# A weight conversion by scaling instead of a range check, and a gather of diagonal blocks on ScalarE alone

## The chip, the cores and the metric

The kernel runs on one core of one Trainium2 chip. The metric is the device time of one execution in microseconds (us). Quoted times are medians of several executions. A profile of one execution stands beside them; its span is about 1.8 us shorter than the time of the same execution. A run counts as fast when it is within 1.5% of the fastest of the same kernel, and each comparison is between fast runs. The experiments ran on five chips; the medians of the kernel before on them lie within 0.3 us of each other, so medians are compared across chips too.

Some terms. *Output products* are the matmuls `p_ffn<-w_out,g`, *solve products* the small ones into `p_one` from `diag` or `r`; each product gives two records in the profile. The *stage* is the stretch from the first to the last `g` of the first two chunks, 78 to 158 us in the kernel before. A *slow phase* is a stretch in which TensorE's granted clock is 0.50; in the 17 traces kept here it is 0.50 or 1.00 and nothing else, and a figure between the two is a mean over a longer stretch.

Engines in profile lines: PE is TensorE, PEld its weight loads, DVE VectorE, ACT ScalarE, POOL GpSimd. "L357" is a line of that kernel's program. The changed kernel has fewer lines, so one operation has different numbers in different kernels: kk is L357 before and L349 after, `low` L562 and L553, `g` L565 and L556.

## The reference

A delta-rule attention (batch 4, 8 heads, 768 steps, head size 48) is followed by a feed-forward layer with a PReLU on 3072 tokens.

```
k_n = k / (norm(k) + 1e-6)
for each step t:   y_t = q_t S
                   S   = S + beta_t * k_t (v_t - k_t S)
h   = y W_in                    # 384 -> 2048
out = (max(h,0) + alpha*min(h,0)) W_out
```

The weights arrive as float64. The chip has to make float32 of them from pairs of 32-bit words.

## The kernel before

The attention is worked in chunks of 64 tokens; 24 steps (12 chunks, 2 halves of the batch). Four steps at a time share one *elimination*: the 32x32 diagonal blocks of `kk` are gathered into `same`, turned by a block transpose, and eliminated row by row on VectorE. TensorE runs the feed-forward products (`ffn_in`, `ffn_out`) between the small products of the attention.

```python
# weight conversion, one piece (cut)
nc.scalar.activation(dst.bitcast(U32), lo, ACT.Copy, scale=2.0**-29)   # low word
nc.scalar.square(lo.bitcast(FP32), hi.bitcast(FP32))                    # for the range check
# VectorE, first half
tensor_scalar(out=high, in0=hi, scalar1=3, scalar2=0x3FFFFFF8, shift_left, and)
scalar_tensor_tensor(out=hi, in0=hi, scalar=0xC0000000, in1=high, and, or)
yield
# second half
tensor_tensor(out=dst.bitcast(U32), in0=hi, in1=dst.bitcast(U32), op=add)
scalar_tensor_tensor(out=dst, in0=lo, scalar=LEAST*LEAST, in1=dst, is_ge, mult)
yield

# prep(n): the weight of each key (cut)
nc.scalar.square(ksq, k)                       # ksq has one buffer
nc.vector.tensor_reduce(out=norm, in_=ksq, op=add)
nc.scalar.sqrt(norm, norm)
nc.vector.tensor_scalar_add(norm, norm, 1e-6)
nc.vector.reciprocal(rec, norm)

# keep(n): gather of the diagonal blocks, right after kk
nc.scalar.mul(same[m][:, j], kk[n][:, :, 0:HB], which[:, 0:1])
nc.vector.scalar_tensor_tensor(out=same[m][:, j], in0=kk[n][:, :, HB:C],
    scalar=which[:, 1:2], in1=same[m][:, j], op0=mult, op1=add)
if j == NJ - 1:                                # every fourth step
    nc.vector.transpose(block[m], same[m])

# ffn_in: after each pair of input products
nc.scalar.activation(low, p_h, ACT.Relu, scale=-1.0)
for i in range(2):
    g[:, i] = low[:, i] * al_t + p_h[:, i]     # VectorE

# the opening, in this order (cut)
busy(31)                                       # filler products while VectorE eliminates
eliminate(0)
weave(ready/pair of steps 0,1 with one filler each, 12 half pieces of the conversion)
weave(steps 2,3; conversion; prep, kk, keep of steps 4 to 7; ffn_in(0))
weave(rest of the conversion; ffn_in(1); kk, keep of steps 8, 9)
weave(eliminate(1), ffn_out(0))
place(4); between_1(4); between_2(4); ...      # first products that need elimination 1
# here the fixed order ends; for the rest the build orders instructions itself
```

`weave` interleaves generators at compile time, so each engine has one fixed row of instructions.

## Time and profile before

| | before |
|---|---|
| median of 3 runs | 795.0 us |
| TensorE busy | 95% of the span |
| VectorE, ScalarE busy | 54%, 27% |
| VectorE busy, 120 to 140 us | 19.1 of 20 us |
| TensorE's granted clock after four waits of 2 to 3 us, mean of 4 us | 0.57 to 0.62 (slow phases of 3.41 us) |

The shares of the whole span name TensorE as the bound; the stretches show another bound, VectorE, between 78 and 160 us. The prediction below shows those lines and reads them.

### The profile page before, as it was taken

What the parts mean: (1) busy time and instruction counts of PE and PEld (TensorE: products, weight loads), DVE (VectorE), ACT (ScalarE), POOL (GpSimd) and SP (SyncE); (2) the same over time, 40 slices, a digit from 0 to 9 for tenths busy, and PEclk for the clock granted to TensorE, in tenths of its full rate; (3) what the DMA queues carried; (4) which work ended last, traced back from release to release, by engine and by line L of the source; (5) the groups of instructions that cost most, each with busy time, mean ns of one, the idle gap of its engine ahead of it and who ended that gap; (6) DMA issues with size and microseconds to landing.
All of it is one profiled execution on the core that took longest, in us unless ns stands there. A gap on an engine that the chain in (4) does not pass through costs nothing.

```text
span 792.7 us, 20343 instructions
## 1 busy us (share of the span) xinstructions
PE 755.3 (95%) x8987; PEld 557.1 (70%) x8987; DVE 429.4 (54%) x1007; ACT 215.4 (27%) x443; POOL 23.3 (3%) x80
## 2 busy tenths in 40 slices
PE   5999888698998999999999999999999999999997
PEld 4457666555787678678678678678677687687684
DVE  6997989995599224596234596223595132122030
ACT  3415546412324123124123123123113122021110
POOL 5000000010000000000000000000000000000000
PEclk9999999999999999999999999999999999999999
DMA  7718453211321122122122121111111110100000
GB/s 154 171 41 223 91 138 82 76 26 32 62 45 34 26 41 42 22 41 42 22 41 41 22 42 31 22 32 32 22 32 31 23 38 3 21 12 2 21 0 21
DMA packets 109417, 37.60 MB, mean 47 GB/s; under 512 B 102625, under 2 KB 105713, under 8 KB 109329
## 3 DMA queue, kind: packets, MB, share of 16 engines
q1 hardware_dynamic: 109296, 36.29, 20.7%
q8 instruction: 71, 1.16, 0.6%
q14 instruction: 18, 0.14, 0.1%
q10 hardware_dynamic: 32, 0.01, 0.0%
HBM read 31.56 MB, written 4.72 MB: 46 GB/s over the span
## 4 chain that ended last, share of the span: by engine, by line
PE 64%; DVE 31%; issue 2%; ACT 2%; POOL 1%; POOLq 0%; DVEq 0%; ACTq 0%
PE p_ffn L584 23%; PE p_ffn L554 20%; DVE block L417 6%; DVE prod L411 6%; PE p_ffn L646 5%; DVE g L565 3%; PE p_one L499 2%; PE p_one L446 2%; PE p_one L513 2%; PE p_big L351 2%; PE p_big L484 2%; PE p_one L457 2%; DVE block L397 1%; DVE turned L422 1%; DVE kk L357 1%
## 5 line engine op out<-in xcount | busy, mean ns | idle before, releaser
L554 PE MATMUL p_ffn<-xt,w_in 128*128 128x256 f32 x1152 | 273.5, 389 | 11.9 <-DVE g L565 6.2
L584 PE MATMUL p_ffn<-w_out,g 128*128 128x384 f32 x768 | 261.1, 492 | 3.9 <-ACT y L492 2.2
L554 PEld LDWEIGHTS p_ffn<-xt,w_in 128*128 128x128 f32 x1152 | 214.9, 192 | 46.3 <-ACT space_out L194 5.8
L584 PEld LDWEIGHTS p_ffn<-w_out,g 128*128 128x128 f32 x768 | 142.5, 191 | 94.3 <-ACT y L492 2.6
L565 DVE SCALAR_TENSOR_TENSOR g<-low,al_t,p_ffn 128x256 f32<-128x256 f32 x192 | 83.4, 476 | 121.2 <-ACT low L562 121.2
L562 ACT ACTIVATE low<-p_ffn 128x512 f32<-128x512 f32 x96 | 56.8, 593 | 106.0 <-PE p_ffn L554 100.8
L411 DVE TENSOR_TENSOR prod<-block 128x30 f32<-128x30 f32 (+9 forms) x180 | 59.4, 330 | 5.6
L417 DVE TENSOR_TENSOR block<-block,prod 128x30 f32<-128x30 f32 (+9 forms) x180 | 59.5, 330 | 5.1
L527 DVE TENSOR_TENSOR y<-y,p_one 128x384 f32<-128x384 f32 x22 | 12.2, 552 | 64.2 <-PE p_one L513 64.2
L449 ACT COPY mid<-p_one 128x256 f32<-128x256 f32 x24 | 8.9, 371 | 102.3 <-PE p_one L446 102.2
L646 PE MATMUL p_ffn<-k_t,ident 128*128 128x512 f32 x76 | 36.3, 625 | 0.0
L590 ACT COPY o_sb<-p_ffn 128x384 f32<-128x384 f32 x24 | 11.5, 478 | 90.6 <-PE p_ffn L584 89.8
L513 PEld LDWEIGHTS p_one<-u,a_t 64*64 64x64 f32 x768 | 24.3, 134 | 12.6 <-issue 8.8
L457 PEld LDWEIGHTS p_one<-diag,mid 64*64 64x64 f32 x768 | 24.3, 135 | 11.1 <-issue 9.4
L487 DVE TENSOR_TENSOR r<-v_raw,p_big 128x384 f32<-128x384 f32 x22 | 11.9, 545 | 36.7 <-PE p_big L484 36.5
L499 PEld LDWEIGHTS p_one<-r,inv 64*64 64x64 f32 x704 | 22.2, 134 | 13.3 <-issue 6.9
L460 DVE TENSOR_TENSOR inv<-diag,p_one 128x256 f32<-128x256 f32 x24 | 10.0, 416 | 35.7 <-PE p_one L457 35.7
L513 PE MATMUL p_one<-u,a_t 64*64 64x48 f32 x768 | 27.2, 220 | 1.3 <-DVE u L501 1.3
L446 PE MATMUL p_one<-diag,kk 64*64 64x32 f32 x768 | 26.4, 220 | 2.1 <-ACT diag L435 2.1
L499 PE MATMUL p_one<-r,inv 64*64 64x48 f32 x704 | 25.0, 220 | 3.3 <-DVE r L487 3.3
L446 PEld LDWEIGHTS p_one<-diag,kk 64*64 64x64 f32 x768 | 24.6, 136 | 3.9 <-ACT diag L435 2.7
L457 PE MATMUL p_one<-diag,mid 64*64 64x32 f32 x768 | 26.9, 220 | 0.0
(101 smaller groups left out, 642.9 us busy)
## 6 DMA issues: line engine op xcount, KB each, us to landing
w_out<-in_moe_w_in_dram SPq DMA_DIRECT2D x12, 512.0 KB, 5.8
kl<-in_k_dram SPq DMA_DIRECT2D x50, 96.0 KB, 3.2
qp<-in_q_dram SPq DMA_DIRECT2D x48, 96.0 KB, 3.0
v_raw<-in_v_dram SPq DMA_DIRECT2D x48, 96.0 KB, 2.8
out_dram<-o_sb SPq DMA_DIRECT2D x48, 96.0 KB, 2.2
ke<-in_k_dram SPq DMA_DIRECT2D x46, 96.0 KB, 3.1
space_out<-in_moe_w_out_dram SPq DMA_DIRECT2D x11, 384.0 KB, 3.6
w_out<-in_moe_w_out_dram SPq DMA_DIRECT2D x5, 384.0 KB, 3.6
```

Of the source, the lines that this page charges most:

```text
L351: nc.tensor.matmul(p[half(t), a, w, g], k_t[n][dims(a), g, half(t)], rhs[n][dims(a), g, half(t)],)
L411: nc.vector.tensor_tensor(out=prod, in0=r[:, 0:j, j : j + 1].to_broadcast([128, j, n]), in1=r[:, j : j + 1, j + 1 : HB].to_broadcast([128, ...
L417: nc.vector.tensor_tensor(out=r[:, 0:j, j + 1 : HB], in0=r[:, 0:j, j + 1 : HB], in1=prod, op=ALU.add)
L446: nc.tensor.matmul(p[half(t), h], kk[n][half(t), h], diag[n % NE][half(t), h, 0:HB])
L457: nc.tensor.matmul(p[half(t), h], mid[n % 2][half(t), h], diag[n % NE][half(t), h, HB:C])
L499: nc.tensor.matmul(p[half(t), h], inv[n % NE][half(t), h], rhs_[n][half(t), h // G, h % G])
L513: nc.tensor.matmul(p[half(t), a, g], a_t[n][half(t), a * G + g], us[n][half(t), a * G + g])
L554: nc.tensor.matmul(p_h[:, i], w_in[:, t, (f + i) * 128 : (f + i + 1) * 128], xt[:, t], start=(t == 0), stop=(t == KT - 1),)
L562: nc.scalar.activation(low, p_h, ACT.Relu, scale=-1.0)
L565: nc.vector.scalar_tensor_tensor(out=g[:, i], in0=low[:, i], scalar=al_t[:, f + i : f + i + 1], in1=p_h[:, i], op0=ALU.mult, op1=ALU.add,)
L584: nc.tensor.matmul(p_o[bp], gs[f // 2][:, f % 2, bp * 128 : (bp + 1) * 128], w_out[:, f], start=(f == 0), stop=(f == FT - 1),)
L646: nc.tensor.matmul(p, ident, k_t[NJ - 1].rearrange("p g i -> p (g i)"))
```

## The change

The intent is to take work off VectorE: one of four conversion steps, one step of each gather, and one small step of each `prep`. A multiplication by 2^-112 on ScalarE re-biases the exponent; a shift then completes the high word. It drops the explicit range check.

```diff
 nc.scalar.activation(dst.bitcast(U32), lo, ACT.Copy, scale=2.0**-29)
-nc.scalar.square(lo.bitcast(FP32), hi.bitcast(FP32))
+nc.scalar.mul(lo.bitcast(FP32), hi.bitcast(FP32), 2.0**-112)
 ...
-tensor_scalar(out=high, in0=hi, 3, 0x3FFFFFF8, shift_left, and)
-scalar_tensor_tensor(out=hi, in0=hi, 0xC0000000, in1=high, and, or)
+tensor_scalar(out=lo, in0=lo, 3, shift_left)
+tensor_tensor(out=dst, in0=lo, in1=dst, op=add)
 yield
-tensor_tensor(out=dst, in0=hi, in1=dst, op=add)
-scalar_tensor_tensor(out=dst, in0=lo, LEAST * LEAST, in1=dst, is_ge, mult)
+scalar_tensor_tensor(out=dst, in0=hi, 0x80000000, in1=dst, and, or)
@@ prep
-nc.vector.tensor_scalar_add(norm, norm, 1e-6)
+nc.scalar.activation(norm, norm, ACT.Copy, bias=1e-6)
@@ keep
-nc.scalar.mul(same[m][:, j], kk[n][:, :, 0:HB], which[:, 0:1])
-nc.vector.scalar_tensor_tensor(out=same[m][:, j], in0=kk[n][:, :, HB:C], ...)
+nc.scalar.copy(same[m][:, j], kk[n][:, :, 0:HB])
+for t in range(2):
+    own = slice(64 * t + HB, 64 * t + C)
+    nc.scalar.copy(same[m][own, j], kk[n][own, :, HB:C])
```

(Names of operations are shortened.)

## The prediction

> **What bounds the kernel now.** I read the busy table first, then the busy time by stretches, the chain of waits between 68 and 200 us, the groups by form, and the order in time of single steps. By the table TensorE is the bound:
>
> ```profile
> PE 755.3 (95%) x8987; PEld 557.1 (70%) x8987; DVE 429.4 (54%) x1007; ACT 215.4 (27%) x443; POOL 23.3 (3%) x80
> ```
>
> The average hides a stage. The change touches the weight conversion (DVE work between 50.7 and 157.8 us) and small steps of the set-up, so the stretches matter. Columns: stretch, length, busy us of PE, PEld, DVE, ACT, POOL, then granted clock, DMA share, GB/s:
>
> ```profile
> 40.00:60.00 20.00, 20.00 (x194) 10.81 (x192) 18.90 (x41) 3.25 (x8) 0.00 (x0) 1.00 0.16 49
> 80.00:100.00 20.00, 16.74 (x331) 13.72 (x330) 18.46 (x41) 10.31 (x22) 1.59 (x4) 0.95 0.39 82
> ...
> 120.00:140.00 20.00, 17.08 (x100) 13.59 (x100) 19.10 (x43) 12.15 (x27) 1.85 (x4) 0.91 0.27 74
> 140.00:160.00 20.00, 14.07 (x87) 10.49 (x88) 17.82 (x40) 9.29 (x19) 0.24 (x1) 0.91 0.29 82
> ...
> 280.00:300.00 20.00, 20.00 (x316) 16.10 (x315) 7.33 (x17) 5.08 (x11) 0.41 (x2) 1.00 0.22 44
> ```
>
> Three regimes are to be seen. Up to about 75 us PE has no gap, because it runs filler matmuls of a fixed number (first line below: 62 records, 28.4 us). From about 78 to 160 us DVE is nearly full and PE has gaps: DVE is the bound. After 260 us PE is full again and DVE has slack. In the chain the middle regime is a row of DVE steps, and the costliest lines are the conversion's own:
>
> ```profile
> 23.40 28.36 PE p_ffn L646 x62
> ...
> by line: DVE g L565 9.6%; DVE block L417 7.6%; DVE prod L411 7.2%; DVE w_out L212 5.3%; DVE w_out L215 5.1%; issue 5.1%; PE p_ffn L584 4.4%; DVE high L202 4.0%; DVE w_out L206 3.9%; PE p_ffn L554 3.8%; DVE space_out L206 3.5%; PE p_one L446
> ```
>
> **What the Trainium skill says.** (1) "ScalarE: Activation LUTs", section "What ACT_TABLE_LOAD costs": an ACTIVATE with immediates takes 186 ns + 0.833 N, each [128,1] pointer operand adds about 93 ns, back-to-back ones overlap by about 93 ns. The trace agrees: L390 (256 elements, pointer scale) takes 507 ns against 492, and starts 0.41 us ahead of its successor. A copy of 256 elements without the pointer is then 0.40 us long and 0.31 us from start to start; no copy of this form is in the trace. (2) "VectorE: DVE Perf Modes", section "The perf-mode tier table": tensor_scalar in fp32 runs at 2x, two-input operations at 1x. Agrees: 512 words take 420 ns in L202 but 679 to 695 ns in L206, L212 and L215. (3) "Advanced Engine Details and Errata", sections "Mode Summary" and "Instruction Support": the second Vector SBUF port is shared with GpSimd, whose instructions and two-port Vector ones block each other; copy, cast and tensor_scalar have the two-port form. Agrees: the first L306 (tensor_scalar on 8 elements) took 2.10 us while GpSimd's memsets ran to 10.34 us; the median of that line is 172 ns. (4) "TensorE: Matmul & The Clock Gate", section "What's actually happening": after an idle window the array runs at half clock. The trace shows a granted clock of 0.57 in 98 to 102 and in 122 to 126 us, 0.58 in 146 to 150 and 0.62 in 186 to 190, each after a PE gap of 2.1 to 3.3 us; gaps of 1.3 and 1.65 us were not followed by it.
>
> **The change part by part: the conversion.** Removed is one of four DVE steps per piece; the shift now works in place on what ScalarE prepared (same 2x form, same ScalarE count), the add and the sign step remain:
>
> ```profile
> L206 DVE SCALAR_TENSOR_TENSOR w_out<-w_out,high 128x512 uint32<-128x512 uint32 x12 | 8.3, 695 | 0.6
> L206 DVE SCALAR_TENSOR_TENSOR space_out<-space_out,high 128x384 uint32<-128x384 uint32 x11 | 6.2, 559 | 0.5
> L391 DVE SCALAR_TENSOR_TENSOR same<-kk,which,same 128x256 f32<-128x256 f32 x24 | 11.6, 483 | 6.1 <-ACT same L390 6.1
> L390 ACT ACTIVATE same<-kk,which 128x256 f32<-128x256 f32 x24 | 12.2, 507 | 38.5 <-DVE kk L357 38.5
> ```
>
> With the five forms of w_out outside the staging space (2.8 us) the sum is 17.3 us. Seven pieces are done before 77.9 us, where PE with its fillers is the bound: nothing from them. After 77.9 us come the second halves of 5 pieces of w_in (0.72 us each with its gap, 3.6 us) and 16 of w_out (0.57 us each, 9.1 us): **12.7 us off DVE's row.**
>
> **The gather of diagonal blocks.** It looks like another 1.1 us six times in this stage: L391 itself, and DVE's 0.58 us wait for ScalarE:
>
> ```profile
> 143.63 0.68 DVE L357 TENSOR_TENSOR kk<-p_big,wgt 128x512 f32<-128x512 f32 x1
> 144.34 0.51 ACT L390 ACTIVATE same<-kk,which 128x256 f32<-128x256 f32 x1 [3.81 <-DVE kk L357]
> 144.76 0.58 ACT L562 ACTIVATE low<-p_ffn 128x512 f32<-128x512 f32 x1
> 144.89 0.48 DVE L391 SCALAR_TENSOR_TENSOR same<-kk,which,same 128x256 f32<-128x256 f32 x1 [0.58 <-ACT same L390]
> 145.37 0.87 DVE L565 SCALAR_TENSOR_TENSOR g<-low,al_t,p_ffn 128x256 f32<-128x256 f32 x2
> ```
>
> But ScalarE works in order, and behind the gather stands `low`, for which DVE's next `g` waits. The build shows this order unchanged, with the second copy waiting for the first. Three copies hold ScalarE 0.44 + 0.31 + 0.31 = 1.06 us instead of 0.41. So `g` comes 0.68 + 0.04 + 1.06 + 0.58 + 0.04 = 2.4 us after kk starts, where it came after 1.74: **a loss of 0.65 us**, not a gain. Going through the six in this stage (at 88.9, 101.4, 112.1, 117.7, 143.6, 151.0): three lose 0.65; one hides 0.25 of a conversion step's saving; one is even, since `low` after copies and two conversion steps comes at the old 3.45 us; the one ahead of the block transpose loses 0.12 (1.15 us of copies against 0.51 + 0.58 with L391). Sum **-2.3 us**.
>
> **The 1e-6 on ScalarE.** Sqrt to reciprocal was 0.45 us with DVE's add between; on ScalarE it is 0.21 + 0.04 + 0.20 + 0.04 = 0.49. DVE waits there either way. But the copy and `low` that follow on ScalarE come 0.23 us later, and where DVE reaches `g` earlier than before this shows: about 0.45 at each of three places (after 82.4, 125.2, 136.7 us), with small ones **-1.8 us**. The stage gains 12.7 - 2.3 - 1.8 = **8.5 us**.
>
> **The start.** The first L306 no longer waits for GpSimd (a reciprocal is not among the two-port forms listed), but wgt is made on GpSimd behind the memsets, at 10.9 instead of 11.2 us; kk(0) gains 0.8 us. Then each round kk, gather, square, reduce, sqrt, reciprocal, kk (2.8 us) takes 0.65 longer through ScalarE. Carried through by hand, the last gather ends 0.55 us later, and the query transposes, which stand behind the copies on ScalarE, some 1.1 us later. With them PE's fixed fillers start later: **+1.1 us**, kept up to 78 us.
>
> **After 160 us.** The second elimination loses three small DVE steps of L306: -0.4. Before 186 us PE waits 2.10 us and then runs cold; this gap shrinks to some 1.5 us, with an even chance that the cold phase (L584 x4 in 2.86 us, else 1.5; L446 1.44, else 1.06: 1.75 us) goes: -0.9. In the main loop only three eliminations with a gather inside get shorter, by 0.4 us of L391; the one PE wait of size there is 2.2 us. One loses 0.13 at its transpose: about -0.8.
>
> Sum: 1.1 - 8.5 - 0.4 - 0.9 - 0.8 = -9.5, so 795.0 - 9.5 = **785.5 us**, 1.2% faster.
>
> **The rivals.** (a) *All of the removed DVE time counts*: 12.7 us and six gathers of 1.1 (one of them still waits), 18 us, 777 us. For it: DVE's row is full from 78 to 160 us. Against: ScalarE's order shown above. (b) *PE takes over at once*, and only its gaps go: 3.26 + 1.32 + 2.92 + 0.98 + 1.06 + 0.84 + 2.82 + 0.73 + 1.65 = 15.6 us in that stage; with the start, 780 us. Against: its 174 input matmuls there cost 0.216 us each at full rate (96 in 20.72 us near the end), 37.6 us, and the other matmuls some 20, so PE has over 20 us of room in 80. (c) *Transfers hold the conversion*: ScalarE already waits 1.15 and 0.73 us for pieces of w_out, since a landing takes 3.3 to 3.6 us after its buffer comes free. Faster DVE asks earlier, but with two pieces between release and use I find 0 to 1.5 us of new waiting: 787. (d) *The start and ScalarE cost more*, if the copies overlap less than the skill says: 0.1 us a copy is 1 us at the start and 1 in the stage: 788.
>
> **Range and chances.** (c) and (d) are likelier in part than (a) or (b). Eight times in ten: 780 to 791 us. Faster by over 2% means under 779.1 us and needs nearly all of (a) or (b): 0.12. Slower by over 2% would need a stage that I have not seen: 0.02. Within 2%: 0.86.
>
> **What would show it.** Right: fillers start some 1 us later (24.3 instead of 23.3); second elimination's first product near 153 instead of 161 us; three ScalarE copies of about 0.4 us per gather and DVE idle ahead of `g` for `low`; the idle put down to L390 gone. Wrong: fillers start no later; DVE goes from kk to `g` in 1.5 us or less (then rival a); PE full from 80 to 160 us (b); ScalarE idle for weight transfers over 3 us (c); a shift of 512 words over 0.6 us, which would take the conversion's gain back.

## The result, and the profile after

The changed kernel took 797.41 us (median of 4 runs, 796.23 to 798.51), the kernel before 794.86 us (4 runs, 793.96 to 795.48) beside it. A ratio in this document is the mean time of one kernel's fast runs over that of the other's fast runs of the same rounds, so it is not quite the ratio of the quoted medians. Here it is 1.0033, with a 95% interval of 1.0015 to 1.005. VectorE's work fell as intended and ScalarE's rose, and the time did not fall. The busy table of the changed kernel:

```profile
PE 757.6 (95%) x8987; PEld 558.7 (70%) x8987; DVE 398.4 (50%) x931; ACT 238.9 (30%) x515; POOL 21.5 (3%) x80
```

The stretches of the changed kernel, with the columns the prediction explains:

```profile
80.00:100.00 20.00, 18.26 (x384) 15.27 (x376) 16.61 (x37) 13.36 (x30) 1.15 (x4) 1.00 0.55 110
120.00:140.00 20.00, 17.72 (x111) 14.63 (x112) 17.87 (x41) 12.93 (x30) 1.22 (x4) 1.00 0.33 90
140.00:160.00 20.00, 16.76 (x92) 11.62 (x91) 14.36 (x39) 12.44 (x31) 2.14 (x7) 0.91 0.36 79
```

VectorE is no longer full there (16.6 us of 20 where it had 18.5), and ScalarE is at 12.4 to 13.4 us. TensorE does more in the same time. So this stage did get faster. Single instructions cost what the prediction had assumed (groups by form of the changed kernel: busy us, mean ns, then idle time ahead of them):

```profile
L385 ACT COPY same<-kk 32x256 f32<-32x256 f32 x48 | 19.3, 402 | 1.0
L388 DVE STREAM_TRANSPOSE block<-same 128x1024 f32<-128x1024 f32 x6 | 12.4, 2065 | 4.8 <-ACT same L385 4.8
L382 ACT COPY same<-kk 128x256 f32<-128x256 f32 x24 | 9.7, 403 | 29.9 <-DVE kk L349 29.9
L207 DVE SCALAR_TENSOR_TENSOR w_in<-w_out,w_in 128x512 uint32<-128x512 uint32 x12 | 8.2, 679 | 0.1
...
L199 DVE TENSOR_SCALAR w_out<-w_out 128x512 uint32<-128x512 uint32 x12 | 5.0, 418 | 0.0
```

The block transpose now waits for the copies, 4.8 us in six transposes. In the kernel before, the same group waited 0.2 us:

```profile
L397 DVE STREAM_TRANSPOSE block<-same 128x1024 f32<-128x1024 f32 x6 | 12.5, 2084 | 0.2
```

**Where the time went.** The start of the same instruction can be compared in two kernels' profiles. Each number below is the start in that kernel's profiled run minus the start in the kernel before; negative is earlier. This table is called the ledger below. Columns e1 to e7 are experiments told further on.

| instruction | before, us | changed | e1 conv. | e2 gather | e3 norm | e4 conv.+norm | e5 conv.+gather | e7 reordered |
|---|---|---|---|---|---|---|---|---|
| first filler | 23.33 | +1.80 | 0.00 | +2.45 | -0.82 | -0.83 | +2.45 | +1.81 |
| first `g` | 77.87 | +1.94 | +0.46 | +2.15 | -1.27 | +0.11 | +3.01 | +2.46 |
| last `g` of the second chunk | 157.67 | -4.99 | -11.88 | +5.15 | -1.00 | -11.13 | -6.24 | -11.48 |
| second elimination's last transpose | 185.58 | -3.88 | -11.90 | +5.17 | -0.49 | -10.66 | -5.56 | -9.96 |
| an attention product of step 5 | 211.65 | -1.88 | -13.27 | +4.06 | +1.08 | -9.59 | -0.62 | -5.28 |
| an output product of chunk 2 | 314.72 | +1.73 | -13.30 | +5.89 | +1.02 | -9.64 | +2.96 | -3.32 |
| last output product | 788.03 | +3.15 | -13.30 | +7.40 | +1.60 | -9.08 | +4.57 | -1.42 |

In the changed kernel the start costs 1.94 us, the stage up to the last `g` gains 4.99 + 1.94 = 6.93 us, and then the kernel loses 4.99 + 3.15 = 8.14 us. The gain did not fail to appear; most of it was given back after 158 us.

**One gather in the changed kernel**, in order of time, the same one as in the prediction (there kk starts at 143.63 us). Columns: start, duration, engine, line, operation, and in brackets the wait before it:

```profile
139.26 0.68 DVE L349 TENSOR_TENSOR kk<-p_big,wgt 128x512 f32<-128x512 f32 x1
...
139.98 0.40 ACT L382 COPY same<-kk 128x256 f32<-128x256 f32 x1 [2.44 <-DVE kk L349]
140.41 0.82 ACT L385 COPY same<-kk 32x256 f32<-32x256 f32 x2
141.25 0.60 ACT L553 ACTIVATE low<-p_ffn 128x512 f32<-128x512 f32 x1
...
141.88 0.87 DVE L556 SCALAR_TENSOR_TENSOR g<-low,al_t,p_ffn 128x256 f32<-128x256 f32 x2 [1.94 <-ACT low L553]
```

`low` stands behind three copies. They hold ScalarE from 139.98 to 141.25, 1.27 us, and VectorE waits 1.94 us for `low`. From kk to `g` it is now 2.62 us; it was 1.74. The prediction had this chain right and made it 2.4 us.

### The profile page after: what moved, and what is told of

Same layout as the page of the kernel before. It is cut to its first block, busy times and chain, and to the rows that moved or that the text cites. A ratio compares the mean times of both kernels' runs of the same rounds, so it can differ in the third digit from the quotient of the medians.

```text
span 795.9 us, 20309 instructions
## 1 busy us (share of the span) xinstructions
PE 757.6 (95%) x8987; PEld 558.7 (70%) x8987; DVE 398.4 (50%) x931; ACT 238.9 (30%) x515; POOL 21.5 (3%) x80
## 4 chain that ended last, share of the span: by engine, by line
PE 65%; DVE 25%; ACT 5%; issue 2%; SPq 1%; DMA 1%; POOL 0%; DVEq 0%; ACTq 0%
PE p_ffn L575 23%; PE p_ffn L545 20%; DVE prod L402 6%; DVE block L408 6%; PE p_ffn L637 4%; DVE g L556 3%; PE p_one L504 3%; PE p_big L343 2%; PE p_one L490 2%; PE p_big L475 2%; PE p_one L437 2%; PE p_one L448 2%; DVE block L388 1%; PE p_big L510 1%; DVE inverse L415 1%
## 5 line engine op out<-in xcount | busy, mean ns | idle before, releaser
L448 PEld LDWEIGHTS p_one<-diag,mid 64*64 64x64 f32 x768 | 24.9, 137 | 11.2 <-issue 8.7
```

Source lines behind the costliest of these rows:

```text
L448: nc.tensor.matmul(p[half(t), h], mid[n % 2][half(t), h], diag[n % NE][half(t), h, HB:C])
```

## The experiments

All outputs are right. Each time stands beside runs of the kernel before on the same chip (medians 794.89 to 795.18 us).

### e1: the conversion alone

Edit: the conversion part of the diff; `prep` and `keep` as before.

> The kernel before with the new weight conversion alone; gather and norm step as before, and the TensorE order in the build is that of before. My theory (the gather and the norm step gave back what the conversion won): the start is as before (fillers at 23.3 us), the second elimination starts some 10 us earlier (149 to 151 us instead of 159.6), and nothing is lost after 186 us: 783 to 787 us. Rival, that removed DVE time is worth little because TensorE or the weight transfers take over at once: 790 to 795 us.

Measured: 781.2 us (780.23 to 781.41), ratio 0.9817 (0.9787 to 0.9848). The stage gained 11.88 + 0.46 = 12.34 us, where the prediction's term is 12.7, and nothing was given back; the time is below the 783 to 787 us of the theory. The granted clock over 160 to 200 us was 1.00 here and 0.96 in the kernel before, and another 1.4 us came from there. From 27 us to the end of its work this profile has no slow phase at all. So the conversion carries all of the gain, and the other two parts lose 16 us between them.

### e2: the gather alone

Edit: the `keep` part of the diff only.

> The kernel before with the gather by ScalarE alone; conversion and norm step as before. The build moves three TensorE matmuls (r with inv) ahead of an output matmul near 254 us, as in the changed kernel. My theory: start 1.5 to 2 us later, 2 to 3 us lost between 78 and 160 us behind ScalarE, 2 to 3 us more at the end of the third elimination (254 to 262 us), about 1.5 us in the three later eliminations: 800 to 804 us. Rival, that the gather is neutral and the loss after 186 us is the norm step's: 794 to 796 us.

Measured: 805.77 us (801.92 to 805.96), ratio 1.0119 (1.0088 to 1.015). The fillers start 2.45 us later. The stage loses 3.0 us, and 2.3 us more follow. This is more than was expected. The profiled run was the fastest of the five, so its ledger understates the median by about 4 us.

### e3: the 1e-6 on ScalarE alone

Edit: the `prep` part of the diff only.

> The kernel before with the 1e-6 added on ScalarE; conversion and gather as before. The build moves one output matmul ahead in the second elimination. My theory: the start wins up to 0.8 us (no wait for GpSimd at 8.3 us), and up to 1 us is lost again through ScalarE: 794 to 796 us. Rival, that the norm step costs the time lost between 186 and 200 us: 797 us or more.

Measured: 795.86 us (792.32 to 799.33), ratio 1.001 (0.9978 to 1.0043). The fillers start 0.82 us earlier, because VectorE's first small step, which took 2.10 us beside GpSimd's memsets, is gone, and the gain is lost again around 160 to 212 us, where the slow phase lasts 6.83 us instead of 3.41.

### e4: conversion and norm

Edit: the diff without its `keep` part.

> Conversion and norm step new, gather as before. If the gather is the whole loss, this is as fast as the conversion alone, within 1 us either way (783 to 787 us). If the norm step takes part of the gain once DVE is faster (each g waits 0.25 us longer for low), it is 1 to 2 us slower than the conversion alone.

Measured: 785.54 us (784.86 to 790.43), ratio 0.989 (0.9859 to 0.9921). Against e1 the norm step costs 4.2 us in the profile: 1.1 us in the stage (12.34 against 11.13 + 0.11 = 11.24), and the larger part after it. That is more than either expectation has. One place shows a part of it. Ahead of the second elimination, the kernel before runs on VectorE:

```profile
158.46 0.55 DVE L304 TENSOR_REDUCE norm<-ksq 128x8 f32<-128x384 f32 x1
159.28 0.17 DVE L306 TENSOR_SCALAR norm<-norm 128x8 f32<-128x8 f32 x1 [0.27 <-ACT norm L305]
159.48 0.20 DVE L308 RECIPROCAL rec<-norm 128x8 f32<-128x8 f32 x1
159.60 1.17 DVE L404 TENSOR_TENSOR block<-block,inside 128x1024 f32<-128x1024 f32 x1
```

and the changed kernel:

```profile
154.08 0.55 DVE L296 TENSOR_REDUCE norm<-ksq 128x8 f32<-128x384 f32 x1 [0.53 <-ACT ksq L294]
155.32 0.55 DVE L296 TENSOR_REDUCE norm<-ksq 128x8 f32<-128x384 f32 x1 [0.69 <-ACT ksq L294]
155.79 0.19 DVE L300 RECIPROCAL rec<-norm 128x8 f32<-128x8 f32 x1
155.90 1.17 DVE L395 TENSOR_TENSOR block<-block,inside 128x1024 f32<-128x1024 f32 x1
```

With the add gone from VectorE, the row is ordered differently: a second reduction stands ahead of the elimination's first step, and it waits 0.69 us for a square on ScalarE. From the start of the first reduction to the elimination it is 1.82 us where it was 1.14. e4 has the same two reductions in a row and the same wait of 0.69 us. By the second elimination's last transpose this has cost e4 0.5 us against e1. Another 2.4 us come between there and step 5's product, where e1 wins 1.37 and e4 loses 1.07: e4 has a slow phase of 6.83 us there, e1 has none. The prediction counted only the three small steps that go away (-0.4 us).

### e5 and e6: the other two pairs

Edit: e5 is the diff without its `prep` part, e6 the diff without its conversion part.

> The changed conversion and the changed gather, with 1e-6 still added on VectorE. Theory 'gather costs what it costs alone' (+7.4 in the profile of the gather-only build, +10.8 in its median): 781.2 + 7.4 to 10.8 = 788.6 to 792.0 us, fillers start at +2.4 us against before, and the stage from the first g to the last g of the second chunk (77.9 to 157.7 us before) gains 12.3 - 3.0 = 9.3 us. Rival 'gather costs more where the conversion is fast, because ScalarE then is what VectorE waits for' (797.4 - 785.5 = 12 us on top of conversion and norm): about 793 us, and the stage gains no more than 7 us.

> The changed gather and the 1e-6 on ScalarE, with the old conversion. If the two add up as they do alone: 805.8 + 0.9 = 806.7 us. If the norm step costs only where VectorE is ahead of ScalarE, which the gather alone does not make it: 804 to 806 us. If the norm's gain at the start (fillers 0.8 us earlier) offsets part of the gather's loss there, as the changed kernel's +1.8 against +2.45 hints: fillers at +1.7 us.

Measured: e5 796.02 us (793.81 to 799.42), ratio 1.002 (0.9994 to 1.0045). e6 803.84 us (803.25 to 806.92), ratio 1.0127 (1.0107 to 1.0146). In e6 the fillers start at +1.81 us as the third expectation has it, and its time is just below the 804 to 806 us of the second: the parts do not add to 806.7. e5 is beyond both theories: the gather costs 14.8 us on top of the conversion (796.0 - 781.2), where alone it costs 10.8 (805.8 - 794.9). The stage of e5 gained 6.24 + 3.01 = 9.25 us, exactly what the first theory says (9.3), so the surplus is not in the stage. It comes after 158 us, where e5 loses 6.24 + 4.57 = 10.8 us. Much of this is the clock: after the last `g`, e5's profile has slow phases of 13.65 and 3.41 us, e4's one of 6.83, and those of the gather alone and of the kernel before one of 3.41 us each. Other runs of e5 had less: three with a mean clock of 0.993 to 0.994 took 793.8 to 794.8 us, three with 0.987 to 0.989 took 797.2 to 799.4. The rival placed the interaction in the stage and falls as well. With the gather in, the norm step costs 1.4 us (797.4 - 796.0) instead of 4.3. Parts do not add, and the places where they interact lie after the stage.

### e7: the same copies, issued behind `low`

Edit, on the changed kernel, for the gathers of steps 4, 5, 6, 8 and 9:

```diff
+held = []                       # gathers not yet issued
 def keep(n):
-    three copies
+    held.append((n, m, j))
+    if not one_of_these_steps: gather()     # at once
 ...
 nc.scalar.activation(low, p_h, ACT.Relu, scale=-1.0)
+gather()                        # the copies that are held, behind low
```

> The whole change, but for the gathers of steps 4, 5, 6, 8 and 9 the three copies are issued on ScalarE behind the next low instead of ahead of it; the work is the same. Theory 'the stage loses because low stands behind the three copies in ScalarE's order': VectorE goes from kk to g without the wait of 0.5 to 2.1 us, the last g of the second chunk comes 4 to 6 us earlier than in the changed kernel, 791 to 794 us in all; the fillers still start at +1.8 us. Rival 'ScalarE is simply too full there, the order does not matter': within 1 us of 797.4.

Measured: 791.95 us (789.72 to 795.22), ratio 0.9971 (0.9949 to 0.9993). The same gather as above, in e7:

```profile
134.64 0.68 DVE L349 TENSOR_TENSOR kk<-p_big,wgt 128x512 f32<-128x512 f32 x1
...
135.24 0.86 DVE L567 SCALAR_TENSOR_TENSOR g<-low,al_t,p_ffn 128x256 f32<-128x256 f32 x2
135.36 0.40 ACT L382 COPY same<-kk 128x256 f32<-128x256 f32 x1 [1.96 <-DVE kk L349]
```

VectorE goes from kk straight to `g` in 0.60 us, and the copies run beside it. The stage gains 11.48 + 2.46 = 13.9 us, 7.0 more than in the changed kernel and 2.7 more than in e4. Slow phases are not what makes the difference here, though the changed kernel has two in the stage and e7 none: e13 has one, e9 and e11 two, and with the changed kernel's order they gain 6.9 to 7.0 us all the same. So the copies cost nothing there as such; their place ahead of `low` did. The Trainium skill says in "Perfetto Trace Analysis", section "Optimizing Scalar/DVE Operations", that offloading from a saturated VectorE to ScalarE may make sense. The trace agrees only for the second order: 13.9 us of stage gain against 6.9, and against 11.2 in e4, where VectorE keeps its step. And of the 6.5 us won up to 158 us, 4.6 reach the end (+3.15 against -1.42), so the part after 158 us was a cause of its own. At the second elimination e7 has 13.65 us of slow clock, the changed kernel 6.83.

### e8: more of the conversion in the stage with fillers

Edit, on e1's kernel:

```diff
-n = 4 * KT            # 12 half pieces
+n = 18
```

> The changed conversion alone, and 18 instead of 12 of its half pieces woven into the stage with fillers (52 to 78 us), where VectorE was idle for 5 us of 52 to 68 us with the conversion changed. If the fillers bind there and VectorE has the room: the last g of the second chunk 3 to 5 us earlier than with 12, 777 to 779 us. Rival 'the transfers of the weights or the free staging places bind': within 1 us of 781.2, with ScalarE or VectorE waiting for transfers before 78 us.

Measured: 782.97 us (780.25 to 783.27), ratio 0.9849 (0.9829 to 0.987). The last `g` came at -14.99, 3.1 us earlier than in e1, as the first theory has it, and the end at -11.24, later than e1's -13.30, so its time missed the 777 to 779 us of that theory. What was won was lost at the second elimination: in both kernels TensorE waits 2.1 us there, and only in e8 it then runs slowly (clock 0.82 over 158 to 186 us, 1.00 in e1). The clock thus decides over some 3 us that no instruction of the edit touches.

### e9: the old gather for the first four steps

Edit, on the changed kernel: `keep` uses the old multiplication and VectorE step for steps 0 to 3.

> The whole change, but the first four gathers (the serial set-up loop) made the old way, by ScalarE and VectorE. Theory 'the gather costs 2.6 us at the start' (the fillers start at -0.83 us with conversion and norm, at +1.80 with all three): fillers at -0.8 us, everything after carries it, 797.4 - 2.6 = 794.8 us. Rival 'what the start loses is hidden later by the wait for the eliminations': within 1 us of 797.4.

Measured: 795.39 us (793.57 to 795.95), ratio 1.0002 (0.9988 to 1.0016). Fillers at -0.83 us, the end at -0.48 instead of +3.15. The start is carried to the end, as the theory says: 2.0 us of median, 3.6 us of profile.

### e10: the old gather from step 8 on

Edit, on the changed kernel: `keep` as before for steps 8 to 23.

> The whole change, but the gathers of steps 8 to 23 made the old way. TensorE's order is then the old one again at the end of the third elimination (three products of the solve no longer stand ahead of the output products). Theory 'that order, with its two waits and the slow clock after them, cost 3.0 us at 250 to 265 us, the three copies ahead of the last three block transposes 1.5 us later, and the copies of steps 8 and 9 up to 1.3 us in the stage': 797.4 - 4.5 to 5.8 = 791.5 to 793 us. Rival 'the waits come back at another place': 796 us or more.

Measured: 792.74 us (791.52 to 793.69), ratio 0.997 (0.9958 to 0.9982), inside what the first theory has. From 211.65 to 314.72 us it loses 0.8 us (-3.77 to -2.99), and nothing later (-3.00 at the end). The changed kernel loses 3.6 us and then 1.4 us in the same stretches. The 1.4 us come in steps around the last three eliminations, whose block transposes wait for copies, and the old gather takes them away. The 3.6 us have three candidates in this run: the copies, TensorE's order, and a slow phase that the changed kernel has there and e10 has not.

### e11 and e13: TensorE's row at the second elimination

Edit, on the changed kernel (e11 with 12, e13 with 14):

```diff
+late = ffn_out(1)
 weave((eliminate(1), HB), (ffn_out(0, True), OUT_PARTS))
+for _ in part(late, 12): pass       # output products of the next chunk, now
 place(NJ); between_1(NJ)
```

The build had put 9 of these products there by itself in the changed kernel and 8 in the kernel before. The later shares are cut accordingly.

> The whole change, with 12 instead of 9 output products of the next chunk ahead of the first product that needs the second elimination (44 instead of 41 in a row); those that follow are fewer. Theory 'TensorE's wait of 2.57 us there and the slow clock after it are what the stage's gain runs into': the wait under 1 us, no slow phase after it, 794 to 796 us. Rival 'VectorE's elimination sets the time there, whatever TensorE does meanwhile': the first product after the elimination at the same time, and no more than 1 us gained.

> The whole change, all copies on ScalarE as changed, with 14 output products of the next chunk ahead of the second elimination's first product (the run before had 12). By the build this also puts TensorE's order at the end of the third elimination to 16 solve products in a row and then 12 output products, where the changed kernel and the run with 12 have 3 solve products, 3 output products, 13 solve products. Theory 'that order, not the copies, makes the loss of about 3 us at 250 to 265 us': no slow phase there, 791 to 793 us. Rival 'the copies make it': 794 to 795.5 us as with 12, and the loss stays.

Measured: e11 794.92 us (793.27 to 795.61), ratio 0.9998 (0.9985 to 1.001). e13 791.39 us (790.69 to 792.27), ratio 0.9942 (0.9911 to 0.9973). TensorE around the second elimination, in the kernel before:

```profile
186.31 1.44 PE L446 MATMUL p_one<-diag,kk 64*64 64x32 f32 x32 [2.10 <-ACT diag L435]
187.67 2.86 PE L584 MATMUL p_ffn<-w_out,g 128*128 128x384 f32 x4
```

in the changed kernel:

```profile
182.43 1.12 PE L437 MATMUL p_one<-diag,kk 64*64 64x32 f32 x32 [2.57 <-ACT diag L426]
183.48 0.91 PE L575 MATMUL p_ffn<-w_out,g 128*128 128x384 f32 x2
184.93 1.64 PE L448 MATMUL p_one<-diag,mid 64*64 64x32 f32 x29 [0.53 <-ACT mid L440]
...
189.20 2.92 PE L575 MATMUL p_ffn<-w_out,g 128*128 128x384 f32 x4
```

and in e13:

```profile
183.51 1.12 PE L437 MATMUL p_one<-diag,kk 64*64 64x32 f32 x32
184.57 0.91 PE L575 MATMUL p_ffn<-w_out,g 128*128 128x384 f32 x2
185.68 1.06 PE L448 MATMUL p_one<-diag,mid 64*64 64x32 f32 x29 [0.20 <-ACT mid L440]
```

The wait of 2.10 us did not shrink to 1.5 us, as predicted; it grew to 2.57 us, with a second one of 0.53 us behind it, since the build had moved one output product from between the two solves to ahead of the first. Four output records still took 2.92 us, at a slow clock. In e11 the first wait is 0.86 us as expected, but the second is 1.31 us and a slow phase follows, so that part of its expectation failed; the first solve product starts at 182.49 us, as its rival has it, and 2.5 us are gained nevertheless, because the three extra output products fill time that was idle. In e13 the first wait is gone and the second is 0.20 us, the clock over 186 to 200 us is 1.00 (0.79 in the changed kernel), and another 3.5 us are gained. Waiting and slow clock at this place are thus worth some 6 us (797.4 - 791.4).

e13 was meant for the *third* elimination. Its time is in the expected range, but **not for the expected reason**: there it still waits 3.05 us and has a slow phase (0.58 over 251 to 255 us).

### The third elimination, from five profiles

The build orders TensorE's row there itself. The kernel before has 3 output products, 16 solve products, 9 output products; the changed kernel has 3 solve products ahead of those; e12, e13 and e15 have 16 solve products and then 12 output products. TensorE in the kernel before:

```profile
256.14 2.17 PE L584 MATMUL p_ffn<-w_out,g 128*128 128x384 f32 x6 [2.23 <-ACT y L492]
```

in the changed kernel:

```profile
253.89 0.43 PE L490 MATMUL p_one<-r,inv 64*64 64x48 f32 x6 [1.18 <-DVE r L478]
256.30 3.65 PE L575 MATMUL p_ffn<-w_out,g 128*128 128x384 f32 x6 [1.98 <-DVE g L556]
```

in e12 and then in e15 (both told below; they have the same row of TensorE):

```profile
239.29 9.67 PE L577 MATMUL p_ffn<-w_out,g 128*128 128x384 f32 x24 [2.94 <-DVE g L558]
```

```profile
238.90 7.98 PE L592 MATMUL p_ffn<-w_out,g 128*128 128x384 f32 x24 [2.95 <-DVE g L573]
```

In the changed kernel the waits are 1.18 + 1.98 = 3.16 us instead of 2.23, and six records take 3.65 us instead of 2.17: 2.4 us together. The first is the order's. The second is the clock's, and not tied to an order: e12 and e15 have the same order and the same wait, and differ by 9.67 - 7.98 = 1.69 us; e7 has the changed kernel's order and its waits (1.20 and 1.97 us), and its six records take 2.17 us. The Trainium skill says in "TensorE: Matmul & The Clock Gate", section "What's actually happening", that the clock follows a free-running window of activity, so that the point of change varies from run to run. These runs agree: equal waits, sometimes with a slow phase that costs about 1.5 to 1.7 us and sometimes without.

What decides can be read from the traces kept. In each of the 17, all changes of the granted clock lie a multiple of 3.41 us apart (in the kernel before at 98.18, 101.60, 122.08, 125.49, 145.97, 149.38, 186.93 and 190.34 us). So a trace falls into windows of 3.41 us, and where these begin is not set by the program: the kernel before, e1 and e8 start their fillers at the same 23.33 us, but their first boundaries come 2.61, 0.12 and 1.00 us after the first instruction. The windows around the wait of 2.94 us in e12 and 2.95 in e15 (columns as in the prediction: stretch, length, busy us of PE first, clock third from the end), first two of e12, then two of e15:

```profile
236.13:239.54 3.41, 0.47 (x9) 0.37 (x6) 3.41 (x6) 2.47 (x6) 0.00 (x0) 1.00 0.19 34
239.54:242.95 3.41, 3.41 (x6) 1.70 (x6) 1.32 (x3) 0.62 (x2) 0.38 (x1) 0.50 0.00 0
```

```profile
233.92:237.34 3.42, 2.03 (x37) 1.52 (x35) 3.35 (x4) 1.81 (x5) 0.00 (x0) 1.00 0.33 58
237.34:240.75 3.41, 1.85 (x6) 1.22 (x7) 3.11 (x7) 2.01 (x5) 0.39 (x1) 1.00 0.03 5
```

In e12 the wait begins 0.22 us after a boundary and lies in one window; TensorE is busy for 0.47 us of it, and the next window is slow. In e15 it begins 2.02 us after one and is divided over two windows, busy for 2.03 and 1.85 us, and no slow phase follows (from 240.75 us the clock stays at 1.00; these boundaries are counted on from e15's change at 25.72 us). So it is in the other pairs: the changed kernel's two waits leave 0.97 us busy in one window, with a slow phase after it, and e7's leave 2.12 and 1.54 us in two, without one; at the second elimination e8's wait of 2.09 us leaves 1.32 us, with one, and e1's of 2.11 us leaves 1.54 and 3.17, without one. Of all windows at full clock up to 770 us, the 33 with TensorE busy for less than 44% were all followed by a slow one, and none of the 3463 with 77% or more; of the 121 between, 7 were, six of them at the second elimination, so the busy share is not the whole rule.

What it costs: from 211.65 to 314.72 us the changed kernel, e5 and e9, with this slow phase, lose 3.6 us each; e7 and the gather alone, with the same order and waits but no slow phase, lose 1.96 and 1.83. The difference of 1.7 us is half of 3.41. At the second elimination the loss goes with the length of the slow phases (the waits before them differ too):

| slow phases, 160 to 202 us | runs | last `g` to step 5's product, against the kernel before |
|---|---|---|
| none | e1, e12, e13, e14, e15 | -1.4 to +0.2 us |
| 3.4 us | before, e2 | 0 and -1.1 us |
| 6.8 us | changed, e3, e4, e9, e11 | +1.5 to +3.6 us |
| 10.2 us | e6, e8, e10 | +2.8 to +3.1 us |
| 13.7 us | e5, e7 | +5.6 and +6.2 us |

A difference of 2 to 5 us between two single profiles of these kernels can therefore be this chance and no effect of an edit.

### e12: an attempt at a better version

Edit, on e8's kernel (conversion only, 18 half pieces early): `BUSY = 29` instead of 31, and 14 output products as in e13.

> An attempt at a better version: the changed conversion with the old gather and the old norm step; 18 half pieces in the stage with fillers; 14 output products of the next chunk ahead of the second elimination's first product; 29 instead of 31 fillers before the first one, which ended about 2 us after the first elimination's transpose. Expected against the conversion alone (781.2 us): 3 us from the conversion woven earlier, which the slow clock near 172 us took away in the run before, and up to 1.8 us from the fillers: 775 to 779 us. Rival 'the times that are saved meet another wait': 780 us or more.

Measured: **777.79 us** (776.0 to 778.15), ratio 0.9779 (0.9764 to 0.9794). TensorE no longer waits at the second elimination and has no slow phase there (busy for all of 158 to 186 us, at clock 1.00). It beats both kernels, and of all runs here only its interval lies wholly below 0.98.

### e14 and e15: two ways to take the gather off VectorE in e12

Edit: from step 4 on, gathers that are not the last of their four are, in e14, one ScalarE copy of 128x256 and two GpSimd copies of 32x256; in e15, for steps 4, 5, 6, 8 and 9, the three ScalarE copies behind `low` as in e7.

> The retuned kernel with the changed conversion alone (777.8 us), where from step 4 on the gathers that are not the last of their four are one ScalarE copy of 128x256 and two GpSimd copies of 32x256. VectorE loses a step of 0.48 us and a wait of 0.58 us for each of five gathers in the stage; ScalarE does no more than before. If VectorE's row is the bound there and GpSimd is free: 3 to 5 us earlier at the last g of the second chunk, 773 to 775 us. Rival 'GpSimd's copies are slow or hold up VectorE, or TensorE is by now the bound': 777 us or more.

> The retuned kernel with the changed conversion (777.8 us in its own run, ratio 0.9779), where steps 4, 5, 6, 8 and 9 gather by three ScalarE copies issued behind the next low, and all other gathers are the old ones. TensorE's order is the same by the build. If the gather is a gain where it stands behind low: VectorE goes from kk to g in 0.6 us instead of 1.75, the last g of the second chunk comes 2 to 3 us earlier than with the old gather (14 us against 11.2 us of stage gain were measured with the norm change in), 775 to 776 us, ratio 0.974 to 0.976. Rival 'weight transfers or TensorE bound the stage by now, as the GpSimd run hinted': 777 us or more.

Measured: e14 777.18 us (776.18 to 779.73), ratio 0.977 (0.9734 to 0.9805); e15 777.91 us (776.11 to 778.69), ratio 0.9778 (0.9748 to 0.9807). Neither differs from e12: both expectations missed, and the rivals stand. In e14 GpSimd's copies took 411 ns each and disturbed nothing that shows, but `g` still waited 0.97 us for `low`, behind one ScalarE copy: kk to `g` 1.66 us where it was 1.74. In e15 kk to `g` fell to 0.60 us, and the last `g` came only 1.5 us earlier (-16.53 against -15.04), because VectorE now waits longer elsewhere: 1.07 and 1.40 us for two other `low`s (0.35 and 0.63 in e12), 0.92 and 1.02 us for other ScalarE work (none in e12). That gain was gone at the second elimination's transpose (-15.16 against -15.04). Shortening VectorE's row by one step no longer shortens this kernel.

## Why the prediction was right or wrong

The predicted sum was -9.5 us; the profile gives +3.15. The difference of 12.65 us splits by the ledger into start, stage, and after 158 us.

| term | predicted | measured | from |
|---|---|---|---|
| start | +1.1 | +1.94 | first `g` |
| stage: conversion | -12.7 | -12.3 | e1 |
| stage: gather | +2.3 | +4.3 | changed kernel against e4 |
| stage: norm | +1.8 | +1.1 | e4 against e1 |
| second elimination | -0.4 | +1.1 | ledger, 157.67 to 185.58 |
| wait and clock before 186 us | -0.9 | +2.0 | ledger, 185.58 to 211.65 |
| main loop | -0.8 | +5.0 | ledger, 211.65 to the end |

The predicted terms add up to -9.6: the prediction's 12.7 - 2.3 - 1.8 is 8.6 and not 8.5. Of its signs, the fillers came 1.8 us later instead of some 1, and the second elimination's first product at 157.2 us instead of near 153.

- **Bound.** Right: VectorE bound the stage from 78 to 160 us, and the conversion alone took 12.3 us out of it.
- **Gather in the stage.** The mechanism was right, `low` behind three copies, and e7 shows it by reversing it. Its size was off: the copies hold ScalarE 1.27 us and not 1.06, as each follows its predecessor after 0.42 us instead of 0.31, and the six gathers lose 0.88, 0.50, 0.63, 0.15, 0.87 and 0.85 us against e1 (kk to `g`), where three had been booked with 0.65 and the other three with 0.4 us together. That accounts for 3.9 of the 4.3 us.
- **Norm in the stage.** About right.
- **Start.** Right in kind, 0.8 us too small; the same 0.1 us per copy would account for it, which was not tested apart. The shortened first round did give 0.8 us (e3).
- **After 160 us.** This is the step that failed: 2.1 us of gain predicted, 8.1 us of loss found, 10.2 of the 12.65 us. It counted instructions that go away and waits that shrink, as if the rows stayed as they were. Three things were missing. The second elimination starts later because VectorE's row was reordered around ScalarE's squares (e4's profile). TensorE's wait for it, which was to shrink to 1.5 us, grew from 2.10 to 3.10 us in two parts, and its slow phase, which was given an even chance to go, grew from 3.41 to 6.83 us (e11 and e13 show what this place is worth). At the third elimination the rows were ordered anew, 0.9 us of waiting and 1.5 us of slow clock came in, and later transposes wait for copies, 1.4 us (e10); 1.2 of the 5.0 us in the main loop are not assigned. The slow phase at the third elimination is chance: the profiled run had it, an equal row in e7 had not.
- **Rivals.** (a) and (b) did not happen. (c) did not happen: ScalarE's waits for weights in the stage fell from 1.15 + 0.73 us to 0.61 + 0.37 us. (d), more cost on ScalarE, was the nearest, but at 788 us still too low, since it too looked only at the start and the stage.
- **Range.** 780 to 791 was too narrow, for it held only doubts about the stage. The class within 2% was right.

What stays open: why a slow phase at the second elimination lasts one window in the kernel before and two to four in others, though TensorE is busy for 13.23 of the 13.65 us of e7's; how often the runs that were not profiled had one; and the rest of e5's loss. After the last `g` e5 loses 6.5 us more than e4 and the gather alone together. Its slow phases there are 10.2 us longer than theirs add up to (each counted against the kernel before), which at half clock is up to 5.1 us.

## What to carry to other kernels

Here a step moved from a full engine to one with room paid only where it stood behind what the full engine waits for next, and in the faster e12 not even there; look at the order on the receiving engine, not at its busy share alone. When a stage gets faster, follow the gain to the next place where the engines meet, because a wait of 2 to 3 us there with a slow clock after it can take back several us. Whether the slow clock follows was a matter of where the wait fell between boundaries 3.41 us apart, so look at the clock of each profile before putting such a difference down to an edit. Do each part of a bundled change alone: here one part of three was worth 1.8%, with retuning around it 2.2%, and the bundle was 0.3% slower.

## What the Trainium skill lacked or had wrong

- "ScalarE: Activation LUTs", section "What ACT_TABLE_LOAD costs": the overlap of about 93 ns did not appear around the copies of 32 partitions. A copy of 128x256 and two of 32x256, 0.40 us each, kept ScalarE 1.27 us from the first to the next instruction, 0.42 us per copy. A shared tile is not the reason: in the changed kernel all 16 instructions of 128 partitions that came straight after a 32-partition copy, on other tiles, `low` among them, began 24 ns after its end. In e14 a copy of 128x256 ahead of `low` took 0.31 us from start to start, as the page has it. The page does not tell the cases apart; whether the number of partitions counts or the partition at which they start was not tested.
- "TensorE: Matmul & The Clock Gate", section "What's actually happening": the page speaks of an idle window of about 3.4 us. Here the clock changed only at multiples of 3.41 us, but the window need not be idle: TensorE was busy for 43% of the window ahead of the slow phase in e10, and for 64% in the changed kernel at the second elimination. So waits of 2.09 us (e8) and 2.94 us (e12) were followed by a slow phase, and equal waits (2.11 us in e1, 2.95 us in e15) were not.
- No page gives the cost of a fp32 copy of 32 partitions: 402 ns on ScalarE and 411 ns on GpSimd for 256 elements, the same as 403 ns for 128 partitions on ScalarE.
